# Two linear-attention blocks on one core: the last two q projections done jointly, by one level of a seven-product scheme

## The chip, the cores and the metric

One core of a Trainium2 chip runs the whole program. A time is the device time of one execution in microseconds (us). The kernel before was timed in three runs; times of single instructions come from one profiled execution.

## The reference

Two independent blocks A and B, each with x of 2048 x 640, are computed and their outputs set side by side:

```python
q, k, v = split(x @ wqkv)                 # 32 heads of 20 features
phi = lambda t: jnp.where(t > 0, t + 1, jnp.exp(t)) + 1e-6
pq, pk = phi(q), phi(k)
kv = einsum("bhsd,bhse->bhde", pk, v)     # per head 20 x 20
z = pk summed over the tokens
o = (pq @ kv) / (pq . z + 1e-6)
out = o @ wo                              # per block 2048 x 640
```

All inputs and outputs are float32.

## The kernel before, in words

**Numbers in two parts.** Every float32 operand of a large product is split into a rounded part ("hi", made by ScalarE with an activation Copy) and the remainder ("lo", made by VectorE with a subtraction, `low`). A product of two such operands is three matmuls: hi x hi, hi x lo, lo x hi (`mm3`, lines 170 to 172, and `product`, line 320).

**Order of the work.** A first phase forms k, the sums over tokens (`gacc`), kv, and the matrices M = kv x wo that replace wo (block B's M reach into the second phase). What concerns the change is the second phase. It works in eight token groups u = 0 to 7 of 512 tokens, groups 0 to 3 of block A and 4 to 7 of block B. For each group there is a **q stage** (`qmm`, `qphi`, `qacc`): five feature chunks c of 128 features, each the sum over five input chunks k of three matmuls with 512 columns, so 75 matmuls, after which ScalarE takes exp and relu of the PSUM bank, VectorE mixes them (`qphi`), and adds the chunk into the denominator's sum (`qacc`, on ScalarE for the first chunk). Then an **o stage** (`outmm`): the group's numerators, divided by the denominator, times M. The o stage already uses a scheme of seven products where eight would be plain (`STEPS`): the token tiles of a group are paired, the features are two pairs of chunks and a fifth chunk, and sums of the operands (`d_sums`) and of the results (`combine`) replace the eighth product. Its 14 steps have 108 matmuls with 320 columns.

The stages run q0, q1, o0, q2, o1, ..., q7, o6, o7: the o stage of a group comes one q stage later, so that its denominator, its division and its splits (`spread`, `invert`, `gather`, `divide`, `d_sums`, `a_split`, `d_split`) are made beside other matmuls. For the last group the denominator comes instead from a matmul with a 0/1 matrix (`denmm`) and a reciprocal of PSUM (`recip`), within o6, since no q stage is left to cover the transfers.

**How the order is set.** Each engine takes its instructions in the program's order. `line` lists all steps of the second phase; after the matmuls of a step, `run` emits what `at` has hung on it, with small offsets from the table `AT` (line 90). `later(n, ...)` puts an instruction off by n steps (a lo part comes a step after its hi part). The tables `SHIFT` and `MOVED` do the same for the first phase. DMAs are issued from SyncE's queue (SP) and, for results and stored parts, from GpSimd's (POOL); a queue stops at a DMA whose buffer isn't free yet, and all behind it wait.

**Inputs of a q stage.** x transposed is loaded from the input (`load_xraw`), its lo part, which the first phase made anyhow, from a DRAM scratch (`load_xq` from `xd`); the hi part, and a quarter of the lo part of two chunks, are made on the core. Staging tiles of 320 KB share seven buffers (`stage`, tag `wst`).

## Time and profile before

| | |
|---|---|
| three runs | 566.07, 567.21, 567.83 us; median 567.21 |
| the profiled execution | 566.22 us, of which the span from the first to the last instruction 564.4 |
| granted TensorE clock | 0.999 of full |
| TensorE matmul busy | 560.2 us, 99% of the span |
| VectorE busy | 424.1 us, 75% |
| ScalarE busy | 329.0 us, 58% |
| GpSimd busy | 84.4 us, 15% |
| moved by DMA | 126.74 MB, mean 225 GB/s |

Busy time of matmuls is counted from start to modelled end. Matmuls overlap, so a group's mean duration is longer than the time by which a matmul delays the next; that time is read from a stage's length and its number of matmuls. In the profile's rows an L with a number is a line of the kernel before. A row that ends in "idle before" tells how long the engine stood still ahead of those instructions, and which instruction ended the wait. Of the second phase, o4 runs from 463.24 us, q6 from 479.08, o5 from 496.11, q7 from 511.95, o6 from 528.97, o7 from 545.29 to 561.11.

### The profile page before, as it was taken

What the parts mean: (1) busy time and instruction counts of PE and PEld (TensorE: products, weight loads), DVE (VectorE), ACT (ScalarE), POOL (GpSimd) and SP (SyncE); (2) the same over time, 40 slices, a digit from 0 to 9 for tenths busy, and PEclk for the clock granted to TensorE, in tenths of its full rate; (3) what the DMA queues carried; (4) which work ended last, traced back from release to release, by engine and by line L of the source; (5) the groups of instructions that cost most, each with busy time, mean ns of one, the idle gap of its engine ahead of it and who ended that gap; (6) DMA issues with size and microseconds to landing.
All of it is one profiled execution on the core that took longest, in us unless ns stands there. A gap on an engine that the chain in (4) does not pass through costs nothing.

```text
span 564.4 us, 9087 instructions
## 1 busy us (share of the span) xinstructions
PE 560.2 (99%) x3231; PEld 512.1 (91%) x3231; DVE 424.1 (75%) x728; ACT 329.0 (58%) x619; POOL 84.4 (15%) x141
## 2 busy tenths in 40 slices
PE   9999999999999999999999999999999999999997
PEld 7989999898989998989888899898989989898997
DVE  5889698886594778878845896968669484856892
ACT  6874667662675875665736764746538363634551
POOL 0111122311011202143110103120011201001010
PEclk9999999999999999999999999999999999999999
DMA  8868789999895786989997985846566994423022
GB/s 281 232 160 232 190 229 314 273 327 356 291 257 149 197 217 121 357 241 245 340 312 248 340 278 196 286 131 225 154 215 215 306 383 147 152 85 112 1 94 93
DMA packets 78613, 126.74 MB, mean 225 GB/s; under 512 B 9768, under 2 KB 40872, under 8 KB 78568
## 3 DMA queue, kind: packets, MB, share of 16 engines
q1 hardware_dynamic: 66120, 86.28, 47.5%
q0 software_dynamic: 12160, 39.66, 25.5%
q8 instruction: 25, 0.41, 0.3%
q10 hardware_dynamic: 288, 0.23, 0.1%
q14 instruction: 20, 0.16, 0.1%
HBM read 73.62 MB, written 49.37 MB: 218 GB/s over the span
## 4 chain that ended last, share of the span: by engine, by line
PE 99%; ACT 1%; DVE 0%; issue 0%; DVEq 0%
PE pa L320 22%; PE pe L320 11%; PE psg L172 8%; PE psg L171 8%; PE psg L170 8%; PE psq L170 8%; PE psq L172 8%; PE psq L171 8%; PE psb L320 7%; PE psk L581 5%; PE pskv L763 2%; PE psm L170 1%; PE psm L172 1%; PE psm L171 1%; PE psi L1097 1%; PE pst L641 0%
## 5 line engine op out<-in xcount | busy, mean ns | idle before, releaser
L170 PE MATMUL psq<-xqh,wqh 128*128 128x512 f32 x200 | 78.4, 392 | 0.0
L172 PE MATMUL psq<-xqh,wql 128*128 128x512 f32 x200 | 78.0, 390 | 0.0
L171 PE MATMUL psq<-xql,wqh 128*128 128x512 f32 x200 | 77.9, 389 | 0.0
L170 PE MATMUL psg<-pkh,xnh 128*128 128x512 f32 x160 | 62.8, 393 | 0.0
L172 PE MATMUL psg<-pkh,xnl 128*128 128x512 f32 x160 | 62.8, 392 | 0.0
L171 PE MATMUL psg<-pkl,xnh 128*128 128x512 f32 x160 | 62.6, 391 | 0.0
L324 ACT ACTIVATE o<-pa 128x320 f32<-128x320 f32 x64 | 28.0, 440 | 53.3 <-PE pa L320 53.2
L548 POOL DMA_DIRECT2D zd<-ek x30 | 26.2, 874 | 130.8 <-DVE ek L540 50.0
L324 ACT ACTIVATE ko<-pa 128x320 f32<-128x320 f32 x52 | 22.4, 434 | 39.7 <-PE pa L320 39.6
L172 PEld LDWEIGHTS psq<-xqh,wql 128*128 128x128 f32 x200 | 37.5, 188 | 7.9
L171 PEld LDWEIGHTS psq<-xql,wqh 128*128 128x128 f32 x200 | 37.6, 188 | 7.4 <-DMA xql<-xd 0.2
L170 PEld LDWEIGHTS psq<-xqh,wqh 128*128 128x128 f32 x200 | 37.6, 188 | 7.3
L931 ACT ACTIVATE pq<-psq 128x512 f32<-128x512 f32 x40 | 23.8, 594 | 29.6 <-PE psq L172 29.4
L172 PEld LDWEIGHTS psg<-pkh,xnl 128*128 128x128 f32 x160 | 30.0, 188 | 7.1 <-DVE xnl L160 0.6
L985 DVE SCALAR_TENSOR_TENSOR pq<-pq,rd 128x1280 f32<-128x1280 f32 x16 | 23.5, 1484 | 16.4 <-DMA rd<-da 16.4
L171 PEld LDWEIGHTS psg<-pkl,xnh 128*128 128x128 f32 x160 | 30.0, 188 | 5.5 <-DVE pkl L556 0.3
L170 PEld LDWEIGHTS psg<-pkh,xnh 128*128 128x128 f32 x160 | 30.1, 188 | 5.2
L933 DVE SCALAR_TENSOR_TENSOR pq<-pq,rq 128x512 f32<-128x512 f32 x40 | 27.5, 687 | 8.6 <-ACT rq L932 8.6
L626 DVE TENSOR_TENSOR gacc<-psg,gacc 128x512 f32<-128x512 f32 (+2 forms) x42 | 25.7, 630 | 9.3 <-PE psg L172 9.2
L552 ACT ACTIVATE pkh<-ek,epst 128x640 fp32r<-128x640 f32 x32 | 25.9, 827 | 10.3 <-DVE ek L540 10.2
L540 DVE SCALAR_TENSOR_TENSOR ek<-ek,ko 128x640 f32<-128x640 f32 x32 | 26.3, 821 | 6.2 <-ACT ko L537 3.7
L416 ACT ACTIVATE ksh<-sx 128x512 fp32r<-128x512 f32 x26 | 16.2, 628 | 24.6 <-DVE sx L434 24.3
(212 smaller groups left out, 1666.1 us busy)
## 6 DMA issues: line engine op xcount, KB each, us to landing
zd<-ek POOLq DMA_DIRECT2D x32, 320.0 KB, 5.4
out<-o POOLq DMA_DIRECT2D x28, 320.0 KB, 3.3
xql<-xd SPq DMA_DIRECT2D x24, 256.0 KB, 4.7
xt<-in_B_xt_tiles SPq DMA_DIRECT2D x16, 320.0 KB, 4.8
xn<-in_B_x SPq DMA_DIRECT2D x16, 320.0 KB, 4.7
xqs<-in_A_xt SPq DMA_DIRECT2D x20, 256.0 KB, 5.8
xqs<-in_B_xt SPq DMA_DIRECT2D x20, 256.0 KB, 5.9
fdmh<-fsh POOLq DMA_DIRECT2D x14, 320.0 KB, 4.5
```

The lines of the kernel that those rows point to most:

```text
L170: nc.tensor.matmul(o, whi, xhi, start=first, stop=False)
L171: nc.tensor.matmul(o, whi, xlo, start=False, stop=False)
L172: nc.tensor.matmul(o, wlo, xhi, start=False, stop=last)
L320: nc.tensor.matmul(o, x, y, start=start and m == r == 0, stop=m == len(terms) - 1 and r == 2, skip_group_check=True)
L324: nc.scalar.activation(x, y, AF.Copy)
L540: nc.vector.scalar_tensor_tensor(ek[n], ek[n], 1.0, rk[n], op0=OP.min, op1=OP.add)
L548: nc.gpsimd.dma_start(zacc[b], e, accum_op=OP.add)
L552: nc.scalar.activation(pk[n][0], ek[n], AF.Identity, bias=epst)
L581: nc.tensor.matmul(kps["c", n][h], plain_x(n, c)[i], plain_w(c)[j][:, h * HF:(h + 1) * HF], start=(c == 0 and i == j == 0), stop=(c == NC ...
L626: nc.vector.tensor_tensor(o, x, o, op=OP.add)
L931: nc.scalar.activation(e, ps, AF.Exp)
L933: nc.vector.scalar_tensor_tensor(e, e, 1.0, r, op0=OP.min, op1=OP.add)
```

## The change

Groups 6 and 7 no longer have q stages of their own. One stage of 46 steps, called r in the list (`qpair`), computes q for both, and the order of the stages becomes ..., q5, o4, r, o5, o6, o7. The 1024 tokens are eight tiles; the even tiles form one half and the odd tiles the other, and "group 6" now means the odd tiles and "group 7" the even ones (the rows of the output are stored accordingly, and `xd` of these tokens is laid out by halves). With the feature chunks 0 and 1 as one half and 2 and 3 as the other, both of the input and of the output, q for chunks 0 to 3 is seven products of halves with results that are summed, in place of eight; the input chunk 4 and the output chunk 4 are done plainly. Every step is three matmuls with 512 columns.

For this the sums of halves have to be formed: those of wq from a second load of wq, as floats (`wsum1`, `wsum2`, `wlast`), split and stored to DRAM (`wsmall`) and loaded into places of wq's split tiles that are no longer needed (`wback`), with two staying on the core (`w23_split`); those of x from loads of x by halves (`load_xs`, `xs_sum`, `xs_split`). The PSUM results are copied and added on ScalarE and VectorE (`keep7`, `copy`, `plus`) ahead of the same exp, relu, mix and sum as before (`phi7`, `mix7`, `acc7`). The denominator by matmul is now that of group 6, within o5; that of group 7 comes by `spread`, `invert`, `gather`, in o5 and o6. Results of o0 to o4 are staged in four parts of one tile that group 7's numerators take over afterwards, those of o5 to o7 in the staging buffers (`oslot`).

The core of the diff (lines of "..." mark what is left out; table entries of `AT` that the text needs are named there; in `SHIFT` fourteen entries go, and in `MOVED` five, none larger than six steps):

```diff
     line = []
-    for u in range(NU + 1):
-        line += [("q", u, c, k) for c in range(NC) for k in range(NC)] * (u < NU)
+    for u in range(NU - 2):
+        line += [("q", u, c, k) for c in range(NC) for k in range(NC)]
         line += [("o", u - 1, s) for s in range(14)] * (u > 0)
+    line += [("r", s) for s in range(46)]
+    for u in range(NU - 3, NU):
+        line += [("o", u, s) for s in range(14)]
     def at(slot, f, *a):
+        if slot[0] == "q" and slot[1] == NU - 2:
+            slot = ("r", NC * slot[2] + slot[3])
         slot = line[line.index(slot) + AT.get((f.__name__,) + a, 0)]
         todo.setdefault(slot, []).append((f, a))
...
+    def oslot(late=False):
+        if late:
+            return stage("o").rearrange("p (a b) -> p a b", a=2)
+        if not ot:
+            ot.extend([q2[0].tile([P, NC, 512], F32, name="o4", tag="o4", bufs=1), 0])
+        k = ot[1] % 4
+        ot[1] += 1
+        return ot[0].rearrange("p c s -> p (c s)")[:, k * D:(k + 1) * D].rearrange("p (a b) -> p a b", a=2)
...
+    def wslots(k):
+        if k == 0:
+            for c in (0, 2, 4):
+                wst["w", 1, c] = stage("wst")
+            wraw["x", 0], wraw["z", 0] = stage("wx"), stage("wz")
+            for c in (1, 3):
+                wst["w", 1, c] = stage("wst")
+        else:
+            wraw["x", 1], wraw["z", 1] = stage("wx"), stage("wz")
+            for a in ("11", "21", "22"):
+                for c in range(2):
+                    xw[a, c] = stage("xs")[:, :512]
+    def wsum1(k):
+        m, n = wst["w", 1, k], wst["w", 1, 2 + k]
+        x = wraw["x", k]
+        tt = nc.vector.tensor_tensor
+        tt(x[:, HQ:2 * HQ], n[:, HQ:2 * HQ], m[:, HQ:2 * HQ], op=OP.subtract)
+        tt(m[:, HQ:2 * HQ], m[:, HQ:2 * HQ], m[:, :HQ], op=OP.subtract)
+    def wsum2(k):
+        m, n = wst.pop(("w", 1, k)), wst.pop(("w", 1, 2 + k))
+        x, z = wraw["x", k], wraw.pop(("z", k))
+        tt = nc.vector.tensor_tensor
+        tt(x[:, :HQ], n[:, HQ:2 * HQ], m[:, HQ:2 * HQ], op=OP.subtract)
+        tt(z[:, :HQ], n[:, :HQ], x[:, :HQ], op=OP.subtract)
+        wraw["T", k] = m[:, :2 * HQ], 1
+        wraw["Z", k] = z[:, :2 * HQ], 0
+    def wlast(k):
+        m = wst.pop(("w", 1, 4))
+        nc.vector.tensor_tensor(m[:, HQ:2 * HQ], m[:, :HQ], m[:, HQ:2 * HQ], op=OP.subtract)
+        wraw["D", k] = m[:, :2 * HQ], 1
...
+    def wsmall(kind, k):
+        t, at = wraw[kind, k]
+        h = [t[:, i * HQ:(i + 1) * HQ] for i in range(2)]
+        nc.scalar.activation(h[1 - at].bitcast(F32R), h[at], AF.Copy)
+        later(1, wsmall_lo, kind, k)
+        later(2, wsmall_store, kind, k)
...
+    def xs_sum(n, c):
+        a11, a21, a22 = (xw.get((a, c)) for a in ("11", "21", "22"))
+        o, x, y, op = {1: (a22, a21, a22, OP.add), 2: (a22, a22, a11, OP.subtract),
+                       3: (a21, a11, a21, OP.subtract), 4: (a22, xw.get(("12", c)), a22, OP.subtract)}[n]
+        nc.vector.tensor_tensor(o, x, y, op=op)
+    RAW = {"S1": "22", "S2": "22", "S4": "22", "S3": "21", "22": "22b"}
...
+    def xs_split(a, c):
...
+        hi, lo = xform(a, c)
+        src = xw[RAW.get(a, a), c]
+        nc.scalar.activation(hi, src, AF.Copy)
+        if a in ("11", "12", "22"):
+            k, t = chunk_of(a, c)
+            nc.sync.dma_start(f32(lo).rearrange("p (j s) -> p j s", s=P), xd[NU - 2][:, k, t])
+        else:
+            later(1, low, lo, src, hi)
...
+    def split_x5(t):
+        r = x5[t] = q2[0].tile([P, 2, 512], F32R, name="x5", tag="sr", bufs=2)
+        nc.scalar.activation(r[:, 0], xw["5", t], AF.Copy)
+        nc.sync.dma_start(f32(r[:, 1]).rearrange("p (j s) -> p j s", s=P), xd[NU - 2][:, NC - 1, t])
...
+    def keep7(c):
+        copy(pq[NU - 1][:, c], half[c])
+    def phi7(u, c):
+        src = got.pop((u, c))
+        e = pq[u][:, c, :]
+        r = got[u, c, "r"] = q1a[0].tile([P, 512], F32, name="rq", tag="rq", bufs=2)
+        nc.scalar.activation(r, src, AF.Exp)
+        nc.scalar.activation(e, src, AF.Relu)
+    def mix7(u, c):
+        e = pq[u][:, c, :]
+        nc.vector.scalar_tensor_tensor(e, got.pop((u, c, "r")), 1.0, e, op0=OP.min, op1=OP.add)
...
+        def prod(a, w, where, ab, first=False):
+            ks = [0] if a in ("15", "25") else [0, 1]
+            for k in ks:
+                (wh, wl), (xh, xl) = wpart(w[0] + k, w[1], ab), xpart(a, k)
+                for r, (x, y) in enumerate(((wh, xh), (wh, xl), (wl, xh))):
+                    nc.tensor.matmul(ps[where, ab], x, y, start=first and k == r == 0,
+                                     stop=k == ks[-1] and r == 2, skip_group_check=True)
+                slot()
...
+        plain5("21", first=True)
+        for ab in range(2):
+            ps["a", ab] = bank("pa", "a")
+            prod("11", (0, 0), "a", ab, True)
+            if ab == 0:
+                pq[u0] = q2[0].tile([P, NC, 512], F32, name="pq", tag="o4", bufs=1)
+            half[ab] = ps["a", ab]
+        plain5("11", first=True)
+        for ab in range(2):
+            ps["e", ab] = bank("pe", "e")
+            prod("S1", (0, 1), "e", ab, True)
+        for ab in range(2):
+            prod("S2", (2, 0), "a", ab)
+            copy(pq[u0][:, 2 + ab], ps["a", ab])
+        for ab in range(2):
+            ps["b", ab] = bank("psb")
+            prod("12", (4, 0), "b", ab, True)
+        plain5("12")
+        for ab in range(2):
+            prod("15", (8, 0), "b", ab)
+            plus(pq[u0][:, ab], ps["b", ab])
+            got[u0, ab] = pq[u0][:, ab]
+        plain5("15", last=True)
+        got[u0, 4] = five[0]
+        for ab in range(2):
+            prod("S3", (2, 1), "a", ab)
+            prod("25", (8, 1), "a", ab)
+            if ab == 0:
+                pq[u1] = q2[0].tile([P, NC, 512], F32, name="pq", tag="pq", bufs=2)
+            copy(pq[u1][:, 2 + ab], ps["a", ab])
+            plus(pq[u1][:, 2 + ab], ps["e", ab])
+            got[u1, 2 + ab] = pq[u1][:, 2 + ab]
+        plain5("25")
+        for ab in range(2):
+            prod("22", (6, 0), "a", ab)
+            prod("25", (9, 0), "a", ab)
+            got[u1, ab] = ps["a", ab]
+        plain5("22", last=True)
+        got[u1, 4] = five[1]
+        for ab in range(2):
+            prod("S4", (4, 1), "e", ab)
+            prod("15", (8, 1), "e", ab)
+            plus(pq[u0][:, 2 + ab], ps["e", ab])
+            got[u0, 2 + ab] = pq[u0][:, 2 + ab]
+        assert n[0] == 46
...
+        if v == NU - 2:
+            w = v - 1
+            chain[v] = [(("o", w, 0), split_acc, v), (("o", w, 3), denmm, v), (("o", w, 3), recip, v, 0),
+                        (("o", w, 4), recip, v, 1), (("o", w, 4), divide, v, 0), (("o", w, 5), divide, v, 1),
+                        (("o", w, 6), a_split, v, 0), (("o", w, 7), d_sums, v, 0), (("o", w, 9), d_split, v, 0),
+                        (("o", w, 10), a_split, v, 1), (("o", w, 11), d_sums, v, 1), (("o", w, 13), d_split, v, 1)]
+        elif v == NU - 1:
+            chain[v] = [(("o", w - 1, 6), spread, v), (("o", w - 1, 11), invert, v), (("o", w - 1, 11), gather, v),
+                        (("o", w, 1), divide, v, 0), (("o", w, 2), divide, v, 1), (("o", w, 3), a_split, v, 0),
+                        (("o", w, 4), d_sums, v, 0), (("o", w, 5), d_split, v, 0), (("o", w, 7), d_sums, v, 1),
+                        (("o", w, 8), a_split, v, 1), (("o", w, 10), d_split, v, 1)]
...
+    for c, i in ((0, 8), (1, 10)):
+        at(("r", i), keep7, c)
+    for u, c, i in ((NU - 1, 0, 28), (NU - 1, 1, 29), (NU - 1, 4, 31), (NU - 2, 2, 32), (NU - 2, 3, 35), (NU - 2, 0, 36),
+                    (NU - 2, 1, 38), (NU - 2, 4, 40), (NU - 1, 2, 47), (NU - 1, 3, 48)):
+        at(back(i), phi7, u, c)
+        at(back(i + 2), mix7, u, c)
+        at(back(i + 3), acc7, u, c)
+    Q, O = NU - 3, NU - 4
+    def spot(i):
+        return ("q", Q, *divmod(i, NC)) if i < NC * NC else ("o", O, (i - NC * NC) // 2)
+    at(("o", O - 1, 4), wslots, 0)
+    for c, a in ((0, ("o", O - 1, 4)), (2, ("o", O - 1, 5)), (4, ("o", O - 1, 8)), (1, ("o", O - 1, 12)), (3, ("o", O - 1, 13))):
+        at(a, load_w, "w", 1, c)
+    for k, (f, *a) in ((k, x) for k in range(2) for x in ((wsum1,), (wsum2,), (wsmall, "T"), (w23_split,), (wsmall, "Z"))):
+        i = [wsum1, wsum2, wsmall, w23_split].index(f) + 2 * (a == ["Z"])
+        at(("o", O - 1, 9 + i) if k == 0 else ("o", O, i), f, *a, k)
+    at(spot(1), wlast, 0)
+    at(spot(2), wsmall, "D", 0)
+    at(spot(3), wslots, 1)
+    for a, c, i in (("11", 0, 8), ("11", 1, 10), ("21", 0, 12), ("22", 0, 31), ("22", 1, 37), ("21", 1, 37)):
+        at(spot(i), load_xs, a, c)
+    for c in range(2):
+        at(("o", O, 4 + c), xs_split, "11", c)
+        at(("o", O, 6 + 3 * c), xs_split, "21", c)
+        at(("o", O, 8 + 2 * c), xs_sum, 1, c)
+        at(("o", O, 9 + 2 * c), xs_split, "S1", c)
+        at(("o", O, 12 + c), xs_sum, 3, c)
+        at(("r", c), xs_sum, 2, c)
+        at(("r", 1), load_xs, "12", c)
+        at(("o", O, 8), wback, "T", c)
+        at(("r", 3 + c), xs_split, "S2", c)
+        at(("r", 9 + c), xs_sum, 4, c)
+        at(("r", 9 + c), xs_split, "12", c)
+        at(("r", 11 + c), xs_split, "S3", c)
+        at(("r", 8 + 5 * c), load_x5, c)
+        at(("r", 14 + 10 * c), load_xs, "22b", c)
+        at(("r", (18, 28)[c]), xs_split, "22", c)
+        at(("r", 21 + c), xs_split, "S4", c)
+        at(("r", 12), wback, "Z", c)
+    at(("r", 12), wback, "D", 0)
+    at(("r", 15), split_x5, 0)
+    at(("r", 20), split_x5, 1)
+    for u in range(NU - 2):
+        for c in range(NC):
             qphi(u, c, qmm(u, c))
             qacc(u, c)
-        if u == NU - 1:
-            close_pool(q1b, "q1b")
-            open_pool(q3, "q3", "right")
         if u > 0:
             outmm(u - 1)
+    qpair()
+    close_pool(q1b, "q1b")
+    open_pool(q3, "q3", "right")
+    for u in range(NU - 3, NU):
+        outmm(u)
```

Offsets in `AT` that move steps named above, in steps of the list: `wslots` of k = 0 by -2, `load_xs` of half 21, chunk 0, by -8, `xs_split` of 11 by +2 and +1, of 21 chunk 1 by +1, of S1 chunk 0 by +3, `xs_sum` 3 by -2 and -1, `xs_sum` 4 of chunk 1 by +7, `d_split` of group 5's second part by -4, `denmm` of group 6 by -1, its two `divide` by +1, its `a_split` by +3 and +2, its second `d_sums` by +1; of group 7 the two `a_split` by +5 and +3 and the first `d_split` by +6.

252 lines of the change are left out of this document (170 added, 82 removed), and 91 rows, old and new, of tables (MOVED, SHIFT).

## The prediction

> **What bounds the kernel now.** I read the page's top first, then TensorE's waits, then the second phase stage by stage.
>
> ```profile
> PE 560.2 (99%) x3231; PEld 512.1 (91%) x3231; DVE 424.1 (75%) x728; ACT 329.0 (58%) x619; POOL 84.4 (15%) x141
> ```
>
> All that TensorE waited for in the whole span is one line, at the start:
>
> ```profile
> PE psi L1097 <- PEq L1565: 0.8, 1, 0.8
> ```
>
> The stages from q5 on, with busy times of each engine, the granted clock, the DMA share and GB/s:
>
> ```profile
> core 0: us, PE busy (x) PEld busy (x) DVE busy (x) ACT busy (x) POOL busy (x), PEclk, DMA share, GB/s
> 446.21:463.24 17.03, 17.03 (x78) 14.09 (x77) 11.90 (x15) 8.70 (x14) 0.59 (x2) 1.00 1.03 372
> 463.24:479.08 15.84, 15.84 (x109) 15.84 (x109) 9.35 (x17) 7.01 (x15) 1.57 (x3) 1.00 0.55 176
> 479.08:496.11 17.03, 17.03 (x78) 14.09 (x77) 14.33 (x19) 8.71 (x14) 0.59 (x2) 1.00 0.49 158
> 496.11:511.95 15.84, 15.84 (x109) 15.84 (x109) 7.01 (x13) 7.01 (x15) 1.57 (x3) 1.00 0.31 100
> 511.95:528.97 17.02, 17.02 (x78) 14.07 (x77) 14.97 (x19) 8.93 (x14) 0.59 (x2) 1.00 0.13 48
> 528.97:545.29 16.32, 16.32 (x113) 16.23 (x112) 13.82 (x22) 7.41 (x16) 1.25 (x3) 1.00 0.10 40
> 545.29:561.11 15.82, 15.78 (x109) 15.52 (x107) 7.69 (x16) 5.79 (x13) 0.91 (x2) 1.00 0.25 96
> 561.11:564.40 3.29, 0.00 (x0) 0.00 (x0) 0.49 (x1) 0.00 (x0) 0.00 (x0) 0.81 0.39 146
> ```
>
> TensorE is busy for all of each stage at full clock, so time is saved only by fewer matmuls, and every wait that the change creates adds in full. The 3.29 us after the last matmul (an addition and the last store) stay. Two more things matter: VectorE already fills 14 to 15 of 17 us of a q stage, and the DMAs are saturated in q5 (share 1.03) but nearly idle from o5 on.
>
> **What the change removes.** Two q stages are 150 matmuls, the stage r is 46 x 3 = 138. One doesn't cost its mean of 389 ns:
>
> ```profile
> L172 PE MATMUL psq<-xqh,wql 128*128 128x512 f32 x100 | 38.9, 389 | 0.0
> ```
>
> A stage of 75 takes 17.03 us, so one delays the next by 17.03 / 75 = 0.227 us, and twelve by **-2.72 us**. That is the whole gain, 0.48% of the time; r lasts 138 x 0.227 = 31.3 us without waits, a step 0.681. The denominator's two matmuls move from o6 to o5, no more.
>
> **What it adds**, and the prices:
>
> ```profile
> L985 DVE SCALAR_TENSOR_TENSOR pq<-pq,rd 128x1280 f32<-128x1280 f32 x10 | 14.9, 1488 | 12.6 <-DMA rd<-da 12.6
> L933 DVE SCALAR_TENSOR_TENSOR pq<-pq,rq 128x512 f32<-128x512 f32 x21 | 14.4, 686 | 1.7 <-ACT rq L932 1.7
> L943 DVE SCALAR_TENSOR_TENSOR acc<-pq,z,acc 128x512 f32<-128x512 f32 x17 | 12.8, 752 | 0.6
> L160 DVE TENSOR_TENSOR dsl<-sr,dsh 128x1024 fp32r<-128x1024 f32 x8 | 9.7, 1218 | 0.0
> L163 ACT ACTIVATE dsh<-sr 128x1024 fp32r<-128x1024 f32 x8 | 8.5, 1061 | 0.0
> L258 ACT ACTIVATE xqh<-xqs 128x512 fp32r<-128x512 f32 x20 | 12.5, 624 | 0.0
> L931 ACT ACTIVATE pq<-psq 128x512 f32<-128x512 f32 x20 | 11.9, 593 | 21.0 <-PE psq L172 21.0
> L324 ACT ACTIVATE o<-pa 128x320 f32<-128x320 f32 x46 | 20.1, 440 | 39.5 <-PE pa L320 39.4
> L327 DVE TENSOR_TENSOR o<-psb,o 128x320 f32<-128x320 f32 x12 | 5.9, 489 | 8.7 <-PE psb L320 8.7
> L1004 DVE TENSOR_TENSOR sr<-pq 128x512 f32<-128x512 f32 x4 | 2.8, 691 | 0.1
> L959 DVE RECIPROCAL rd<-psd 128x256 f32<-128x256 f32 x2 | 3.5, 1757 | 0.9 <-PE psd L954 0.9
> L970 DVE TENSOR_TENSOR da<-da 128x256 f32<-128x256 f32 x4 | 1.7, 420 | 2.5 <-DMA da<-acc 2.5
> L971 DVE TENSOR_TENSOR da<-da 128x128 f32<-128x128 f32 x4 | 1.2, 292 | 0.1
> L972 DVE RECIPROCAL da<-da 128x128 f32<-128x128 f32 x4 | 3.8, 954 | 0.1
> ```
>
> VectorE's instructions start a little before the last one's end:
>
> ```profile
> 467.26 0.75 DVE L943 SCALAR_TENSOR_TENSOR acc<-pq,z,acc 128x512 f32<-128x512 f32 x1
> ...
> 518.40 0.68 DVE L1008 TENSOR_TENSOR sr<-pq,sr 128x512 f32<-128x512 f32 x1
> 519.00 0.68 DVE L1009 TENSOR_TENSOR sr<-pq 128x512 f32<-128x512 f32 x1
> ```
>
> so each counts for 0.08 us less in a sequence. Additions of a PSUM bank of 512 columns on VectorE, and its copy on ScalarE, aren't in these rows: between the 0.42 of 256 columns and the 0.75 of an `acc`, I take 0.69.
>
> *VectorE from o4 to the middle of r.* Its last `acc` of q5 ends at 468.0, 4.8 us into o4; the three new 256-column steps in q5 (wlast and two lo parts) fit into that stage's free 5.1 us. From there to the lo part of group 5's first `d_split` (step r12) stand in its queue: six operations of 256 columns (wsum, lo parts of T and Z), 6 x 0.42 = 2.5; fourteen of 512 (w23's lo part, six lo parts of x, seven sums of x) and the four of `d_sums`, 18 x 0.69 = 12.4; six `plus` of o4, 2.9; `invert`, 0.42 + 0.29 + 0.95 = 1.7; two `divide`, 3.0; two lo parts of 1024, 2.4. That is 24.9 in 37 instructions, less 37 x 0.08: 21.9 us. Where a lo part waits for its hi part made just then, I add 1.2 (two 0.6 ScalarE operations; bounds 0 and 2.5). VectorE gets there at 468.0 + 21.9 + 1.2 = **491.1**, without one wait for a DMA. What hangs on it: `split_x5` puts its tile into the buffer (tag `sr`) which that lo part frees, so SP issues the load of x5's lo part only then; TensorE needs it in step 22, at 479.08 + 22 x 0.681 + 0.23 = 494.3. The landing times in the quiet stretch of q6 and o5 (478 to 512):
>
> ```profile
> out<-o POOLq DMA_DIRECT2D x5, 320.0 KB, 2.7
> xqs<-in_B_xt SPq DMA_DIRECT2D x5, 256.0 KB, 5.9
> xql<-xd SPq DMA_DIRECT2D x3, 256.0 KB, 2.9
> xql<-xd SPq DMA_DIRECT2D x2, 128.0 KB, 3.5
> ```
>
> A load on its own takes 2.9, five at once 5.9. With 2.9 and 0.5 for SP's queue the part lands at 494.5: a wait of **+0.2**, 0 to 3.2 over the two rows. If VectorE were never held up the term would be 0; it is the nearest thing to a bound that r has.
>
> [...]
>
> *The two loads behind a store.* The buffers of x's halves 22 and 21 of chunk 1 come free when T of wq has been stored. T's lo part is VectorE's fifth operation after 468.0, done at 469.7; issue and store 2.7, load (second in its queue, 0.4) 2.9: 475.7. VectorE comes to `xs_sum` 1 of chunk 1, the first to need it, after 17 instructions (8.9 - 1.4) and those 1.2, at 476.7. So 1.0 us in hand, cost 0, and what is behind that `xs_sum` on VectorE is the whole list above. SP stops at the first of these two loads, and behind them stand the lo part of half 11 (needed at r2), group 5's `gather` and the loads of T; ScalarE stops at the hi part of 21. With a load of 5.9 and the store as it was in 430 to 530,
>
> ```profile
> out<-o POOLq DMA_DIRECT2D x12, 320.0 KB, 3.6
> ```
>
> the data come at 479.6, 2.9 late.
>
> *VectorE and ScalarE in o5.* Group 6's denominator starts at o5's step 2: TensorE is through `denmm` at 3 x 0.88 + 0.46 = 3.1 us (six 320-column matmuls 0.88, from 15.84 / 108). Then VectorE runs in order two `recip` 3.5, `mix` and two `acc` of group 7 2.2, two `divide` 3.0, five `plus` (of steps 6 to 9 and 12) 2.4, two `d_sums` of two instructions each 2.8, two lo parts of 1024 2.4, `invert` 1.7: 18.0 in 21 instructions, less 1.7, so the second `d_sums` is done 3.1 + 0.1 + 16.3 = 19.5 us into o5. ScalarE's queue then has `d_split`'s hi part (1.06), and behind it the copy of o6's first product (0.44), which TensorE's step 4 of o6 must await before it accumulates into the same bank: 19.5 + 1.0 + 0.44 = 20.9. TensorE is there at 15.84 + 0.46 + 4 x 0.88 = 19.8. A wait of **+1.1**; if all starts without the overlap, 2.8; if VectorE's list is a us shorter than I read it, 0. The two `plus` ahead of o5's step 12, behind `divide`, cost **+0.2** (0 to 0.5).
>
> *The rest.* ScalarE in r: 20 exp and relu 0.6, 6 copies, 12 hi parts 0.62, group 5's splits 4.4, about 26 of 31 us; it waits for VectorE, not the other way. Group 7's `a_split` and `d_split` in o6 end just ahead of o7 by the same prices: 0, with o6's matmuls as the cover, and about 1 if that is late. The first phase's moved entries shift steps that TensorE didn't wait for: 0, within 0.3 either way.
>
> **Sum:** -2.7 + 0.2 + 1.1 + 0.2 = -1.2. The profiled execution, 566.2, becomes 565.0; the median of the runs, 567.2, stands 1.0 higher, so **566.0**. What this kernel's measurement can tell from no change is 0.3%, 1.7 us.
>
> **The rivals.**
>
> *No waits at all.* If VectorE's list in o5 is short enough, the whole 2.7 us arrive: 564.5. For it: VectorE's sequence in o6 before, just as dense (13.82 of 16.32), left TensorE no wait. Against it: the queue order above has `d_split` ahead of the copy. A quarter.
>
> *Late loads, slower.* If the loads of r behave like the five at once, 5.9, the chain from T's store makes VectorE 2.9 late at 476.7, all of its list moves with it, and x5's lo part takes 3.0 longer on top: +0.2 + 2.9 + 3.0 in r, +1.3 in o5 and o6, -2.7: +4.7, 571.9; halfway, 569.5. It decides from the point where the store and load together pass 6.6 us, for 5.6 in the quiet rows. For it: r issues some 20 loads within 15 us, and those of x now have pieces of 512 bytes, which in the row of 128 KB took 3.5. Against: q6, o5 and q7 show shares of 0.49 to 0.13, so the queues were empty. [...]
>
> *The weights' second load delays M.* Five loads of wq, 1.6 MB, go in front of M's loads in o3 and q5, at 372 GB/s 4.4 us. M's part 8 was issued at 455.5 and lands 6.1 later:
>
> ```profile
> 455.50 0.51 SPq L906 DMA_DIRECT2D f<-fdmh x1
> ...
> f<-fdmh SPq DMA_DIRECT2D x1, 320.0 KB, 6.1
> ```
>
> With 4.4 that is 466.0, and o4's step 6 needs it at 463.24 + 5.28 = 468.5. 2.5 us in hand; if the new stores (0.8 MB, 2.1 us) and the smaller ones eat that, TensorE waits up to 2: 568.0.
>
> **How the numbers follow.** Forecast (own range 565.1 to 567.9) 0.43; no waits 0.25; late loads 0.24; M late 0.08. Faster by over 0.3%, below 565.5: no waits, and an eighth of the forecast: 0.31. Slower, above 568.9: most of the late loads, a little of M: 0.24. Between: 0.45. Range 564.4 to 570.0: it holds the first two cases, M late, and the late loads up to somewhat past half way.
>
> **What would show it.** Right: 3219 matmuls, r with 138; TensorE waits of a few tenths in r on x5's lo part, and about 1 us on the copy of `pa` in o6. Wrong: no wait in o6 (then my list for o5 is too long), waits at r's steps 1 or 12 (then T's store and the two loads were late), waits in o4 on M. If TensorE's waits exceed 4.4 us the kernel is slower by over 0.3%; under 1 us it is faster.

## The result, and the profile after

The kernel after takes **571.8 us** (median of four runs, 571.07 to 572.80); the kernel before, run beside it, 566.8 (566.07 to 567.83). The ratio is 1.0088, with a 95% interval of 1.0065 to 1.0112: it is slower. The profiled execution has 571.82 us and a span of 570.0, 5.6 more than before. Twelve matmuls are gone, worth 2.7 us, so TensorE waits 8.3 us that it didn't wait before.

The top of the page, and TensorE's waits (us in total, times, longest):

```profile
PE 561.5 (98%) x3219; PEld 508.7 (89%) x3219; DVE 441.1 (77%) x755; ACT 338.8 (59%) x635; POOL 87.2 (15%) x146
```

```profile
PE pe L341 <- DVE o L348: 1.4, 3, 0.6
PE pa L1247 <- ACT pq L345: 1.2, 1, 1.2
PE psi L1365 <- PEq L1886: 0.8, 1, 0.8
PE psb L1247 <- DMA x<-xd: 0.6, 1, 0.6
PE ps L175 <- DVE xql L164: 0.2, 1, 0.2
...
PE pa L341 <- ACT o L345: 0.2, 1, 0.2
```

3219 matmuls, as the change says. VectorE's busy time rises by 17.0 us (424.1 before), 27 instructions more. The list of waits has seven lines that it didn't have before (all but `psi`; the "..." stands for two of the first phase), but it holds only half of the time, 4.0 us, since it counts a wait from the modelled end of the matmul before. What a place costs is read from the stages. Here is the answer for the stages of the kernel after, from q5 on: q5, o4, r, then o5 to o7 together, then the tail.

```profile
core 0: us, PE busy (x) PEld busy (x) DVE busy (x) ACT busy (x) POOL busy (x), PEclk, DMA share, GB/s
0.00:447.56 447.56, 445.58 (x2573) 405.48 (x2573) 343.71 (x609) 275.40 (x517) 76.67 (x127) 1.00 0.82 247
447.56:464.76 17.20, 17.20 (x78) 14.01 (x76) 14.62 (x23) 10.23 (x19) 2.96 (x6) 1.00 0.99 351
464.76:481.04 16.28, 16.11 (x109) 15.85 (x108) 14.00 (x26) 7.05 (x17) 1.62 (x3) 1.00 0.88 277
481.04:515.86 34.82, 32.79 (x140) 25.60 (x139) 31.07 (x46) 25.25 (x45) 1.62 (x3) 1.00 0.54 171
515.86:566.71 50.85, 49.81 (x327) 47.78 (x325) 37.23 (x52) 20.83 (x39) 4.32 (x8) 1.00 0.22 79
566.71:570.00 3.29, 0.00 (x0) 0.00 (x0) 0.49 (x1) 0.00 (x0) 0.00 (x0) 1.00 0.40 149
```

Here a stage begins with its first matmul. For the kernel before, the stage bounds given ahead of the result lie about 0.15 us late (no length changes by more than 0.07); q5's first matmul there:

```profile
446.06 0.39 PE L170 MATMUL psq<-xqh,wqh 128*128 128x512 f32 x1
```

Against the stages of before, read the same way, and with r's 138 matmuls at 0.227 (17.03 us / 75) as its length without waits:

| | up to q5 | q5 | o4 | r | o5 to o7 |
|---|---|---|---|---|---|
| without new waits | 446.06 | 17.03 | 15.84 | 31.33 | 48.10 |
| after | 447.56 | 17.20 | 16.28 | 34.82 | 50.85 |
| waits | 1.50 | 0.17 | 0.44 | **3.49** | **2.75** |

They sum to 8.35. Of the 1.50, 0.86 stands at o3's end; the rest is scattered over the first 440 us, by amounts in which executions differ anyway (the first experiment below, which equals the kernel before up to there, comes to q5 0.82 later than before). Note the DMA share too: 0.88 in o4, which had 0.55 before, and 0.54 in r, where q6 and o5 had 0.49 and 0.31.

VectorE of the kernel after, the rows that answer to the prediction's list (start, duration; at the end the idle time before it and what ended it):

```profile
443.98 0.43 DVE L1014 TENSOR_TENSOR da<-da 128x256 f32<-128x256 f32 x1 [2.74 <-DMA da<-acc]
...
448.37 0.43 DVE L1099 TENSOR_TENSOR wx<-wst 128x256 f32<-128x256 f32 x1 [1.91 <-DMA wst<-in_B_wq]
...
469.96 0.75 DVE L981 SCALAR_TENSOR_TENSOR acc<-pq,z,acc 128x512 f32<-128x512 f32 x1
...
478.25 0.69 DVE L1163 TENSOR_TENSOR xs<-xs 128x512 f32<-128x512 f32 x1 [0.61 <-DMA xs<-in_B_xt]
...
481.25 0.69 DVE L1163 TENSOR_TENSOR xs<-xs 128x512 f32<-128x512 f32 x1 [1.31 <-DMA xs<-in_B_xt]
...
494.55 1.22 DVE L164 TENSOR_TENSOR dsl<-sr,dsh 128x1024 fp32r<-128x1024 f32 x1
```

The list starts at 470.7, not 468.0, waits 2.1 us in it (0.61 and 1.31 for halves of x, 0.15 for ScalarE), and group 5's first lo part of `d_split` ends at 495.8, not 491.1. ScalarE stands behind the late sums of x, and the copy that TensorE needs in r's step 12 stands behind ScalarE's next hi parts:

```profile
488.67 1.24 ACT L1179 ACTIVATE xqh<-xs 128x512 fp32r<-128x512 f32 x2 [5.50 <-DVE xs L1163]
489.81 1.04 ACT L167 ACTIVATE dah<-pq 128x1024 fp32r<-128x1024 f32 x1
490.76 0.58 ACT L345 ACTIVATE pq<-pa 128x512 f32<-128x512 f32 x1
```

The loads, from the answers on the DMA issues of 463 to 480 us:

```profile
xs<-in_B_xt SPq DMA_DIRECT2D x6, 256.0 KB, 5.7
xql<-xd SPq DMA_DIRECT2D x2, 256.0 KB, 5.9
...
wdT<-wst POOLq DMA_DIRECT2D x1, 256.0 KB, 2.9
```

The single store of T, 256 KB issued from GpSimd, took 2.9 us; the six loads of x, as large each, beside one another and issued from SyncE, took 5.7.

And the end of o5, VectorE and then TensorE:

```profile
532.50 0.42 DVE L1014 TENSOR_TENSOR da<-da 128x256 f32<-128x256 f32 x1
...
535.09 0.69 DVE L1053 TENSOR_TENSOR sr<-pq 128x512 f32<-128x512 f32 x1
535.69 0.48 DVE L348 TENSOR_TENSOR o<-pe,o 128x320 f32<-128x320 f32 x1
```

```profile
536.23 0.42 PE L341 MATMUL pe<-fh,dsh 128*128 128x320 f32 x1 [0.45 <-DVE o L348]
```

The last `plus` of o5 stands behind group 7's `invert` and group 6's second `d_sums`, and o6's step 3 needs its bank. The time from a matmul's start to the next, less 0.147 (15.84 us / 108), gives 0.23 behind o5's `denmm`, 0.32 later in o5, 0.25, 0.72 and 0.11 us in o6's first steps, 0.66 near o6's end and 0.40 in o7. The two longest, 0.72 and 0.66, are by their rows waits for a `plus` (0.45 and 0.40 there, counted from the modelled ends).

### The profile page after: what moved, and what is told of

Read it like the earlier page. It is cut to its first block, busy times and chain, and to the rows that moved or that the text cites. A ratio compares the mean times of both kernels' runs of the same rounds, so it can differ in the third digit from the quotient of the medians.

```text
span 570.0 us, 9167 instructions
## 1 busy us (share of the span) xinstructions
PE 561.5 (98%) x3219; PEld 508.7 (89%) x3219; DVE 441.1 (77%) x755; ACT 338.8 (59%) x635; POOL 87.2 (15%) x146
## 3 DMA queue, kind: packets, MB, share of 16 engines
HBM read 77.09 MB, written 50.68 MB: 224 GB/s over the span
## 4 chain that ended last, share of the span: by engine, by line
PE 68%; DVE 12%; DMA 8%; issue 5%; ACT 3%; SPq 2%; POOL 0%; DVEq 0%; POOLq 0%; ACTq 0%
PE pa L341 15%; PE pe L341 7%; PE psg L176 7%; PE psg L175 7%; PE psg L174 7%; PE psk L602 5%; PE psb L341 5%; PE psq L174 4%; PE psq L176 4%; PE psq L175 4%; DMA wst<-in_B_wq 2%; PE pskv L784 2%; DMA xs<-in_B_xt 2%; DMA da<-acc 1%; DVE dsl L164 1%
## 5 line engine op out<-in xcount | busy, mean ns | idle before, releaser
L174 PE MATMUL psq<-xqh,wqh 128*128 128x512 f32 x150 | 59.1, 394 | 0.0
L176 PE MATMUL psq<-xqh,wql 128*128 128x512 f32 x150 | 58.5, 390 | 0.0
L175 PE MATMUL psq<-xql,wqh 128*128 128x512 f32 x150 | 58.4, 389 | 0.0
L176 PEld LDWEIGHTS psq<-xqh,wql 128*128 128x128 f32 x150 | 28.2, 188 | 6.0
L174 PEld LDWEIGHTS psq<-xqh,wqh 128*128 128x128 f32 x150 | 28.2, 188 | 5.7 <-ACT xqh L279 0.3
L175 PEld LDWEIGHTS psq<-xql,wqh 128*128 128x128 f32 x150 | 28.2, 188 | 5.4
L577 DVE SCALAR_TENSOR_TENSOR pkl<-ek,pkh 128x640 fp32r<-128x640 f32 x32 | 25.9, 820 | 5.7 <-ACT pkh L573 5.7
L967 DVE SCALAR_TENSOR_TENSOR pq<-pq,rq 128x512 f32<-128x512 f32 x30 | 20.6, 687 | 8.5 <-ACT rq L966 8.5
```

The costliest lines, as they stand in the source:

```text
L174: nc.tensor.matmul(o, whi, xhi, start=first, stop=False)
L175: nc.tensor.matmul(o, whi, xlo, start=False, stop=False)
L176: nc.tensor.matmul(o, wlo, xhi, start=False, stop=last)
L577: nc.vector.scalar_tensor_tensor(lo, ek[n], EPS, f32(hi), op0=OP.add, op1=OP.subtract)
```

## The experiments

Theory A: late transfers (T's store and the loads behind it, the second load of wq, short pieces of x). Theory B: VectorE's list is too long, whatever the transfers do. All runs in one table; times are medians, ratios are to the kernel before beside them, with 95% intervals, and the last columns are stage lengths of the profiled execution, worked out from the first matmuls of each stage (where nothing was changed they still differ, by up to 0.9 us: o5 to o7 in e2, q5 in e3 and e8).

| | time | ratio | q5 | o4 | r | o5 to o7 |
|---|---|---|---|---|---|---|
| after | 571.8 | 1.0088 (1.0065 to 1.0112) | 17.20 | 16.28 | 34.82 | 50.85 |
| e1 before, 12 matmuls fewer | 562.9 | 0.9939 (0.9923 to 0.9956) | | | | |
| e2 no second load of wq | 569.6 | 1.0066 (1.0043 to 1.0089) | 17.03 | 15.84 | 33.50 | 51.77 |
| e3 x in long pieces | 570.9 | 1.0087 (1.0066 to 1.0109) | 18.05 | 16.28 | 33.82 | 51.00 |
| e4 both, and no stores and loads back | 568.6 | 1.0040 (1.0027 to 1.0054) | 17.05 | 15.85 | 32.63 | 50.08 |
| e5 before, new order tables | 566.6 | 1.0004 (0.9993 to 1.0014) | | | | |
| e6 no stores and loads back | 568.8 | 1.0042 (1.0026 to 1.0059) | 17.03 | 15.96 | 32.55 | 50.78 |
| e7 sums on GpSimd | 578.1 | 1.0199 (1.0175 to 1.0224) | 17.77 | 19.83 | 38.72 | 50.89 |
| e8 other order at o5's end | 570.4 | 1.0060 (1.0042 to 1.0079) | 18.04 | 16.25 | 35.60 | 50.17 |
| e9 T of chunk 1 in place | 568.9 | 1.0056 (1.0035 to 1.0077) | 17.07 | 16.21 | 33.03 | 50.81 |
| e10 d_split first | 570.1 | 1.0079 (1.0058 to 1.0099) | 17.05 | 15.85 | 33.66 | 50.88 |
| e12 M's load back | 574.0 | 1.0149 (1.0131 to 1.0166) | 22.56 | 15.84 | 32.40 | 50.22 |
| e11 e8 + e9 + e10 + e12 | 571.7 | 1.0098 (1.0075 to 1.0121) | 21.65 | 15.84 | 31.92 | 50.61 |
| e13 e9 + e10 + part of e8 | 569.9 | 1.0065 (1.0048 to 1.0082) | 17.04 | 15.85 | 32.66 | 50.68 |
| e15 sums of wq later, M's load back | 576.6 | 1.0185 (1.0170 to 1.0200) | 18.00 | 21.54 | 34.47 | 50.66 |
| e14 e13 + e15 | 574.0 | 1.0143 (1.0128 to 1.0158) | 17.95 | 21.87 | 32.48 | 50.60 |
| e17 e8 + e9 + e10 | 569.4 | 1.0060 (1.0041 to 1.0079) | 17.03 | 15.85 | 32.11 | 50.86 |
| e16 e17, no second load of wq | 569.6 | 1.0057 (1.0039 to 1.0076) | 17.04 | 15.85 | 33.07 | 50.41 |
| e18 e6 with a shorter list on VectorE | 566.3 | 1.0007 (0.9990 to 1.0024) | 17.04 | 15.84 | 31.58 | **48.73** |

**The gain by itself (e1).**

```diff
-            mm3(ps, wh[:, cs], wl[:, cs], xh, xl, k == 0, k == NC - 1)
+            if u >= NU - 2 and (k == 1 or (c, k) == (2, 3)):
+                nc.tensor.matmul(ps, wh[:, cs], xh, start=False, stop=False)
+                nc.tensor.matmul(ps, wh[:, cs], xl, start=False, stop=False)
+            else:
...
```

> The kernel before with twelve matmuls left out of q6 and q7 (the product wlo x hi in six of the 25 steps of each; that part of q is not computed). It measures the gain by itself. If a matmul that goes is worth 0.227 us, as the stage length says, the time is 2.7 us below the kernel before: about 564.1. If the gain was the step that failed (the engines beside TensorE take over), the time stays above 565.5.

Its q stages, the columns as above:

```profile
479.75:495.41 15.66, 15.66 (x72) 12.96 (x70) 11.50 (x15) 7.98 (x13) 0.75 (x2) 1.00 0.53 169
511.25:526.92 15.67, 15.67 (x72) 12.97 (x71) 13.09 (x17) 8.70 (x14) 0.76 (x2) 1.00 0.17 60
```

17.03 has become 15.66, 2.7 us in the two. The median falls by 3.0, by the interval 2.5 to 4.4: the gain was priced rightly, and the loss lies in what the change adds.

**The transfers (e2, e3, e4, e6).**

```diff
 # e2: load_w("w", ...) returns at once; wsum1, wsum2, wlast read whl["q", 1, k][0] (the hi parts)
 # e3: xspan
-    [... (NG - 2) * 512:].rearrange("p (j t s) -> p t j s", t=2, s=P)[:, t]
+    [... (NG - 2 + t) * 512:(NG - 1 + t) * 512]
 # e6: wsmall_store without nc.gpsimd.dma_start, wback returns at once;  e4: all three
```

> The kernel after without the second load of wq (1.6 MB in o3 and q5); the sums of wq are formed from the hi parts that are on the core already, so the lo parts are missing in them. Every other instruction and transfer stays. Theory 'saturated q5' (the five loads delay group 4's spread, the sums of q5 and with them VectorE's list by 2.7 us): the waits of 1.3 us at the end of o3 and in o4 go, and most of the 3.1 us in r: 568 to 569. Theory 'late loads in r': only the 1.3 us go, about 570.5. Theory 'lists of VectorE and ScalarE too long': the same 570.5, with the waits at r's steps 1, 12 and 22 and in o5 and o6 where they were.

> The kernel after with the halves of x loaded as 512 neighbouring tokens, rows of 2 KB, in place of every second tile, pieces of 512 bytes (the hi parts are then of other tokens). Same bytes, same order. If the short pieces are what makes those loads land after 5.7 and 4.1 us, they land after about 3 and r's waits on them and behind them shrink by 2: about 569.8. If it is the number of transfers under way, the time stays at 571.8 within 0.5.

> The kernel after without the second load of wq (as in the run before but one), with x in long pieces, and without the stores of T, Z and D and their loads back (TensorE multiplies with the old parts of wq there, so q is not that of the reference). All matmuls and all work of VectorE and ScalarE stay; only SP's load of x and its lo parts is left of the new transfers. If late transfers are the cause (both theories on DMAs), r and o4 run without waits: 564.5 to 566.5. If the lists of VectorE and ScalarE are the cause, r still waits at steps 12 and 22 and o5 to o7 for their 2.6 us: 569 or more.

> The kernel after without the stores of T, Z and D and their loads back (TensorE multiplies with the old parts of wq there, so q is not the reference's); the second load of wq and the short pieces of x stay. Theory 'T's store holds up the two loads of x behind it': the wait of 1.5 us at r's step 12 and the 0.75 at its start go, 569.5. Theory 'the second load of wq and number of transfers': those two waits stay within 0.5, since the list starts 2 us late already: 571.3 or more.

Long pieces changed nothing in the time (1.0087; the six loads then took 5.2 us, not 3): the size of the pieces is out as the main cause. Without the second load of wq the waits in o4 and at r's start are gone, but the interval still meets that of the kernel after. Without the stores and loads back the time falls to 1.0042, as far as with all three (1.0040):

```profile
464.21:480.17 15.96, 15.96 (x109) 15.85 (x108) 15.43 (x29) 8.82 (x20) 1.08 (x2) 1.00 0.77 232
480.17:512.72 32.55, 31.97 (x141) 25.76 (x140) 29.17 (x43) 23.34 (x41) 1.08 (x2) 1.00 0.41 131
512.72:563.50 50.78, 49.77 (x327) 47.73 (x325) 37.20 (x52) 20.84 (x39) 4.33 (x8) 1.00 0.22 79
```

r is 2.3 us shorter, o4 0.3; o5 to o7 are as long as ever. So theory A holds for about 2.6 us of r and o4 (2.6 by the time too, 1.0 to 4.2 by the two intervals), and neither it nor the second load explains the rest. What is left of it in e4 is VectorE's own list, as its busy time from its last `acc` of q5 to the end of group 5's splits shows, 26.69 of 27.40 us:

```profile
469.70:497.10 27.40, 26.61 (x144) 23.60 (x143) 26.69 (x44) 16.53 (x31) 2.16 (x4) 1.00 0.64 199
```

**T's store (e9), and the buffer of x5's lo part (e10).**

```diff
 # e9: wsmall, for T of chunk 1; its wback returns at once
+        split(*(y[:, HQ:2 * HQ] for y in whl["q", 1, 1]), h[at])
 # e10: AT
-    ('d_split', 5, 1): -4,
+    ('d_split', 5, 0): -2, ('d_sums', 5, 1): 3, ('d_split', 5, 1): -4,
```

> The kernel after with T of chunk 1 written straight into its place in wq's split tiles (these are no longer read once q5 is over), without its store and its two loads back; the buffer it lay in, where a half of x is loaded next, is free as soon as its lo part is made. All else stays. Theory 'T's store holds up the loads of x and through them VectorE's and ScalarE's queues': most of what leaving out all stores and loads back brought (the waits at r's start and step 12, and in o4): 2 us less, 569.8. Rival 'the many small transfers together, not this chain': a third of it at most, 571.

> The kernel after with group 5's first d_split ahead of its second d_sums on VectorE (and two places earlier on ScalarE), so that the buffer for x5's lo part comes free some 1.8 us earlier. If VectorE's list up to that lo part sets the wait at r's step 22, its 0.85 us goes and nothing else changes: 571.0. If step 22 waits for something else behind it (ScalarE's copy, the next load), the wait moves by a step or two and the time stays at 571.8.

One store and two loads less give r 33.03 (1.8 us less) and a time of 1.0056, whose interval still meets that of the kernel after. VectorE's waits for loads of x in its list fall from 1.92 us (0.61 and 1.31 above) to 0.34, and to none in e6: by the stages, T's chain is the larger part of what e6 gained. In e10 the wait for x5's lo part (0.86 by the start-to-start times) is gone, and a new one of 0.57 stands ahead of it, for ScalarE's second copy of `pa`. r is 1.2 shorter, but 0.76 of that is the wait at r's start, ahead of the moved instruction: in that execution VectorE waited only 1.08 us for those loads of x, with T's store and loads in place, so the size of T's chain differs between executions too. The time (1.0079) can't be told from the kernel after.

**The order tables (e5).** `SHIFT` and `MOVED` of the kernel after and four entries of `AT`, put into the kernel before.

> The kernel before with the order tables of the kernel after: SHIFT and MOVED whole, and of AT the four entries for steps that both have (a_split, d_sums and divide of group 4, form_load 1 1). No other part of the change, the same matmuls. In the kernel after about 0.5 us of small waits stand ahead of o3 and 0.85 at o3's end, also without the new transfers. If the order is their cause, this kernel has them: 566.8 + 1.3 = 568.1. If they come from the new work itself, it stays at 566.8 within 0.5.

1.0004 (0.9993 to 1.0014): by the time they cost nothing that can be seen, which leaves room for 0.8 us. Its trace has 0.43 us of waiting at o3's end all the same. One of the four entries, `form_load` by -5, puts a load of M ahead of group 4's `spread` in SyncE's queue, and VectorE's `invert` waits longer for it. The row of the kernel before, then that of e5:

```profile
441.64 0.42 DVE L970 TENSOR_TENSOR da<-da 128x256 f32<-128x256 f32 x1 [1.02 <-DMA da<-acc]
```

```profile
442.76 0.43 DVE L968 TENSOR_TENSOR da<-da 128x256 f32<-128x256 f32 x1 [2.31 <-DMA da<-acc]
```

It is 2.74 in the kernel after and 2.54 in e2, which has no second load of wq and 0.67 us of waiting at o3's end. So most of that wait comes with the moved load of M, not with the second load of wq.

**o3 and q5 (e12, e15).**

```diff
 # e12 and e15: AT
-    ('form_load', 1, 1): -5,
 # e15 also
+    ('wsum1', 0): 4, ('wsum2', 0): 4, ('wsmall', 'T', 0): 4, ('w23_split', 0): 4, ('wsmall', 'Z', 0): 4,
+    ('wlast', 0): 4, ('wsmall', 'D', 0): 4,
```

> The kernel after with form_load of M's part 1 at its old place (the entry -5 in AT taken out), so that its 320 KB are not in front of group 4's spread. The wait at o3's end (0.85, behind an addition that stands in VectorE's queue behind group 4's invert, which waited 2.7 us for the spread) goes if that load delays the spread: 571.0. If the spread is late because of the halves' and wq's loads, or M's part then comes too late for o4, the time stays at 571.8 or rises.

> The kernel after with the sums of wq's first chunk, their splits and stores (wsum1, wsum2, wsmall, w23_split, wlast) four steps later, in q5 in place of the end of o3, and M's load at its old place. Theory 'the wait at o3's end, and the 3.7 us in q5 that came up when M's load went back, both hang on VectorE and ScalarE standing in their queues for the second load of wq': both go, 570.5 to 571. Rival 'M's loads and those of wq are too many bytes for o3 and q5 in any order': TensorE waits in o3, q5 or o4 for 1 us or more all the same, 571.5 or more.

Both are slower. With M's load back, the wait at o3's end is gone (group 4's spread lands earlier), but the second load of wq is late instead; `wsum1` waits, ScalarE's hi part of T behind it, and the hi part of x that q5 needs behind that. q5 is 5.5 us longer than in the kernel before: 3.9 are the wait itself and the first matmul behind it, to whose successor it is 0.33 us (452.06 to 452.39) and not 0.227. The rest comes from the eight matmuls from 452.89 to 456.27, 0.42 us apart in the mean, as in e7 at a granted clock of 0.50 (see the last section). TensorE's wait, and ScalarE's row:

```profile
PE psq L174 <- ACT xqh L279: 3.7, 1, 3.7
```

```profile
451.07 0.42 ACT L1131 ACTIVATE wst<-wst 128x256 fp32r<-128x256 f32 x1 [7.56 <-DVE wst L1100]
```

In e15 nothing stands in the queue there any more, and now group 4's gather is late, so that its division and its splits keep o4 waiting:

```profile
454.71 2.90 DVE L1029 SCALAR_TENSOR_TENSOR pq<-pq,rd 128x1280 f32<-128x1280 f32 x2 [7.27 <-DMA rd<-da]
```

So none of the three orders is free: with M's loads and wq's together in o3 and q5 (DMA share 0.99 in q5 of the kernel after), each of them makes something else late. The change's order, with 0.86 us at o3's end, is the best of the three. M's load at its old place without the second load of wq was not run.

**The end of o5 (e8).**

```diff
+    ('invert', 7): 1, ('gather', 7): 1, ('d_split', 6, 1): 2,
-    ('d_sums', 6, 1): 1,
+    ('d_sums', 6, 1): 2,
```

> The kernel after with another order on VectorE at the end of o5: the two last additions of o5 (plus) go ahead of group 7's invert and group 6's second d_sums, and on ScalarE the hi part of d_split behind the copies of o6's first two products. Theory 'TensorE waits at o6's steps 2 and 3 for those additions': the 0.3, 0.7 and 0.1 us there go: 1.1 less, 570.7. Theory 'the list is too long whatever its order': group 7's gather is 0.5 later, o6 and o7 wait instead, and the time stays at 571.8 within 0.4.

The 0.25, 0.72 and 0.11 are gone, but further on o6 waits 0.96 (0.70 in the row) for the lo part that was put back, and o5 to o7 is only 0.7 shorter:

```profile
542.75 0.41 PE L341 MATMUL pa<-fh,dsl 128*128 128x320 f32 x1 [0.70 <-DVE dsl L164]
```

The time (1.0060) fell by more than that, but two intervals of 0.2% either way are as wide as the difference.

**Together (e11, e13, e14, e16, e17).**

> T of chunk 1 in place, the earlier d_split of group 5, M's load at its old place and the other order at the end of o5, together on the kernel after. If the causes are separate, their parts add: 2.0 + 0.85 + 0.85 + 1.1 = 4.8 less, 567.0, the same as before. If the gain of one is the cover of another (a wait that goes lets the next one appear), 568.5 or more.

> The kernel after with T of chunk 1 in place, group 5's first d_split earlier, and the other order at the end of o5 (the hi part of d_split behind the copy of o6's first product only); M's load stays where the kernel after has it. If these three causes are separate, their parts add: from 1.0088 down by 2.0 + 0.85 + 1.0 us to about 1.002, 568 us or 1.2 above the kernel before. If they cover one another, 1.004 or more.

> All of the two runs before this one in one kernel. If the causes add: about 1.002 less another 0.85 to 1.3 us, 566.6 to 567.2, no slower than the kernel before; the waits left are the 0.4 ahead of o3 and 0.9 in o5 to o7. If the second load's delay only moves on into o4 and r, 568 or more.

> T of chunk 1 in place, group 5's first d_split earlier, and at the end of o5 the order of e8 (the hi part of d_split behind the copies of both first products of o6, whose lack cost e13 1.7 us there). If the parts add, from 1.0088: 1.8 + 0.5 + 1.0 us less by what each of these gave alone, 1.003, 567.6 to 568.2; if they cover one another, 1.005 or more.

> The run before this one, and without the second load of wq (sums from the hi parts on the core, their lo parts missing). If the four causes (T's store, the buffer of x5's lo part, the order at the end of o5, the second load in saturated queues) are all there is, TensorE's waits from o3 on fall from 7.4 us to under 2.5, and the kernel is no slower than before, 565.5 to 567. If the change's work on VectorE and ScalarE alone eats the twelve matmuls, 567.5 or more.

They don't add up. Those with M's load at its old place (e11, e14) lose it all again in q5 or o4. e13 put the hi part of `d_split` ahead of one copy of `pa`, and there TensorE waited 1.83 us in o6 for that copy, the second product's; the prediction had named the first's, for the same reason. e17 avoids this, has 2.7 us less in r than the kernel after, and is no faster than e9 alone. None of them beats the kernel before. Taking the second load away as well (e16) brings nothing more.

**VectorE's work (e7, e18).**

```diff
 # e7: wsum1, wsum2, wlast, xs_sum
-        nc.vector.tensor_tensor
+        nc.gpsimd.tensor_tensor
 # e18: e6, and for x's sums and halves and for groups 5, 6, 7 the hi part in place of the lo part
-            later(1, low, lo, src, hi)
+            xf[a, c] = [hi, hi]          # the same in a_split and d_split
```

> The kernel after with the sums of wq and of x (nine of 256 columns, seven of 512) on GpSimd in place of VectorE; no trace shows GpSimd's price for them. Theory 'VectorE's list is the bound from o4 to r': VectorE has 9 x 0.34 + 7 x 0.61 = 7.3 us less to do, the waits for x5's lo part (0.85) and at r's step 12 (1.5) go or shrink: 569 to 570. Rival 'the sums are a chain, not a load': GpSimd takes longer for each, the hi parts behind them on ScalarE come later, and r waits more: 572 or more.

> The run without stores and loads back (e6), and also without VectorE's lo parts of x's halves and of the splits of groups 5, 6 and 7 (TensorE multiplies with the hi parts in their place; the same matmuls). VectorE has some 20 us less to do from o4 to o6, about 8 of them ahead of x5's lo part. Theory 'what stays after the stores are gone is VectorE's list': the wait at r's step 22 (0.85) and those in o5 to o7 (2.0) go, 2.5 to 3 us under e6's 1.0042: 0.998 to 1.000, no slower than the kernel before. Rival 'it is ScalarE, or waits scattered over the whole run that no list explains': 1.003 or more.

GpSimd is no place for these sums: r grew to 38.7 (see the last section). e18 leaves out, besides e6's stores and loads back, VectorE's lo parts of x's sums and halves and of the splits of groups 5 to 7; ScalarE's work stays (23.63 and 20.73 us against 23.34 and 20.84). It decides. Its page, TensorE's waits and the last stages:

```profile
PE 557.7 (99%) x3219; PEld 508.9 (90%) x3219; DVE 421.9 (75%) x730; ACT 338.7 (60%) x635; POOL 84.5 (15%) x141
```

```profile
PE pe L341 <- DVE o L348: 1.0, 1, 1.0
PE psi L1372 <- PEq L1893: 0.8, 1, 0.8
```

```profile
479.56:511.14 31.58, 31.58 (x141) 25.91 (x140) 20.16 (x29) 23.63 (x43) 0.89 (x2) 1.00 0.42 133
511.14:559.87 48.73, 48.67 (x327) 47.74 (x325) 27.98 (x42) 20.73 (x39) 4.31 (x8) 1.00 0.23 82
```

With 9.0 us less on VectorE in r and 9.2 in o5 to o7 than e6 has, r is within 0.3 of its 31.33 and o5 to o7 within 0.6 of 48.10. In the list of waits only that at o3's end is left, which none of this touches. It is the one kernel of all that shortens o5 to o7 by more than executions differ, by 2.05 us against e6. What TensorE waited for there in the longest places, a `plus`, is still made in e18, only sooner, so in o5 to o7 the cause is the length of VectorE's list. In r, 1.0 shorter than in e6, the list and a dependence can't be told apart: without the lo part of `d_split`, the buffer for x5's lo part comes free after ScalarE's hi part already. By the time e18 is at 1.0007, 0.35% or 2.0 us under e6 (0.6 to 3.3 by the two intervals). That is a little above the 0.998 to 1.000 expected, and its interval ends below the rival's 1.003. Its profiled execution, 565.2 us, is among its fastest, and what the others lost isn't in a trace.

## Why the prediction was wrong

The forecast was 566.0 with 1.5 us of waits, the range ended at 570.0; measured were 571.8 and 8.3 us.

- **The gain, 2.7 us: right** (e1: 2.7 in the stages). The order tables at 0: right by the time (e5), but not in the trace. The entry that moves M's load had no term in the sum, and it makes most of the 0.86 us at o3's end: 0.43 by itself (e5), none with the load back at its place (e12).
- **VectorE's list up to x5's lo part: the sum right, its start wrong.** Worked out were 23.1 us; it took 495.77 - 470.71 = 25.1, less its 2.1 us of waits 23.0. The equal sum is partly luck: the instructions took 23.0 where 21.9 was worked out, and of the 1.2 added for ScalarE's hi parts 0.15 came. But the step "Its last `acc` of q5 ends at 468.0 ... fit into that stage's free 5.1 us" took the clock of the old trace. The stage began 1.7 us later, and the list began 5.95 us into it, not 4.93. Without the second load of wq it began at 5.04 to 5.06 (e2, e4, e16); with it, at 5.07 where VectorE waited 0.87 us for it (e18) and at 5.96 where it waited 2.76 (e3), so the late start within the stage is that load's. The later start and the waits in the list turn the 0.2 put down for x5's lo part into 0.86 (start to start).
- **T's store and the two loads, "1.0 in hand, cost 0": the step that failed most.** Its rows came from q6 and o5 of the kernel before, and the argument "so the queues were empty" from their DMA shares. In the kernel after these queues carry the change's own transfers. T's lo part was done at 472.8 where 469.7 was worked out, and store and load took 8.5 us, not 6.0. The store was priced nearly right (2.9 for 2.7); the load, issued at 476.00 and awaited until 481.25, took 5.2 with its queue behind other loads, where 3.3 were put down. VectorE had come 3.2 us late as well, so the wait in it was only 1.3, but ScalarE, which then stood 5.5 us for VectorE's next sums of x, came late to the copy, and that made the 1.2 us at step 12 (1.5 start to start). Cost: 1.8 us of r by e9, 2.3 with the other stores and loads back (e6).
- **o5 and o6, +1.3: mechanism right, place and size wrong.** VectorE's second `d_sums` of group 6 ended 19.9 us into o5 (535.78 - 515.86), predicted 19.5. But TensorE stopped earlier than at the copy: at o5's last `plus`, which the prediction didn't look at behind the same instructions. And the list doesn't end there: near o6's end and in o7, both put at 0, TensorE waits again. Together 2.75 against 1.3; e18 shows the cause, e8 that another order helps little.
- **M late: not as put.** TensorE never waited for M's parts. The second load of wq, counted there with 4.4 us, delayed the list's start instead, by 0.9 us (e2), and in e2 the waits at r's start and the 0.6 in q5 and o4 are gone too. They are also gone in e10, where VectorE waited for that load 1.22 us in place of 1.91.
- **The rival "late loads", 571.9, met the time but not the reason.** It had 6.1 us in r (3.5 measured), 1.3 in o5 and o6 (2.75 to o7's end) and nothing ahead of r (2.1). Its mechanism is there, with 2.6 us (e6; most of it T's chain, by e9's stages); the equal sum is chance.

Of the marks that were given, those for "wrong" came: waits at r's steps 1 and 12, and more than 4.4 us in all. Of the 8.3 us, 2.6 are the stores and the loads behind them (e6, by the stages and by the time), 3.0 by the stages or 2.0 by the time are VectorE's list (from e6 to e18; of the 3.0, the 1.0 in r may be the buffer), 0.86 stand at o3's end. How the remaining 1.9 share out between executions that differ, q5 and what e18 still waits isn't settled.

## What to carry to other kernels

Twelve matmuls were bought with 17 us on VectorE, which in r is then busy for 31.1 of 34.8 us; a list of 25 us with hardly a gap passes on every delay ahead of it, and mending one place shows the next. A price for a transfer has to come from the queues as the change will leave them: add its own loads and stores to the stage's DMA share before calling a queue empty. When several mends each shorten a stage and the time doesn't follow, look for the engine whose work none of them made less.
